# Linear attention and a gated FFN on one core: one written list for the order of all queues, one ring of PSUM banks, loads reordered, zero matmuls at the start

## The chip, the cores and the metric

The kernel runs on one core of a Trainium2 chip. The metric is device time in microseconds of one execution; lower is better. The median of three runs of the kernel before is 246.35 us (245.84 to 247.32). A core has TensorE (PE, matmuls), VectorE (DVE), ScalarE (ACT), GpSimd (POOL) and SyncE (SP). Each runs its own queue of instructions in order; they meet through semaphores. Here POOL issues the loads that have to be cast to fp16 on their way (and some others), SP the remaining loads, the DMA transposes and the stores.

## What is computed

```python
# q, k, v: (8, 8, 576, 64) float32
q_s = softmax(q, axis=-1)            # over the 64 features
k_s = softmax(k, axis=2)             # over the 576 positions
kv  = einsum('bhsd,bhse->bhde', k_s, v)
att = einsum('bhsd,bhde->bhse', q_s, kv)
x   = att.transpose(0, 2, 1, 3).reshape(4608, 512)
h   = (x @ w1) * (x @ w2)            # w1, w2: (512, 1024)
out = (h @ w3) @ w_out               # w3: (1024, 1024), w_out: (1024, 512)
```

## The kernel before, in words

**Fold.** w3 @ w_out is computed once (W3O, 1024 x 512), so that the second half of the FFN is one product. For each of eight row blocks `ft`: `w3t.ft` transposes eight 128x128 blocks of w3 on TensorE (L441), `w3T.ft` copies them from PSUM to SBUF, `pf.ft.0` and `pf.ft.1` are two times four matmuls with w_out (L451), and `W3O.ft` evicts the sum.

**Attention, for each batch b.** Steps are named by their kind, the batch and a part:
- `kmx`, `cb`: maximum of k over the positions, on VectorE (L479, or a tree at L488 to L491 in batches 0 and 1; `cb` is L495 to L506). `ksub` (L537) subtracts it, `kexp` is the exponential on ScalarE. There are two halves, `.0` and `.1`.
- `vc` casts v to fp16 (batches 2 to 7). In batches 0 and 1 the load casts.
- `kv` is the product of k's exponentials and v on TensorE (L562, L571), `kv2` its normalisation (L580 to L583).
- `qmx` (L590), `qsub` (L595), `qexp` (L603), `qsm` (L608), `qeps`, `qrc` (L620), `qn` (L627): softmax of q in two parts of 4 and 5 groups of positions (`.0` and `.1`).
- The result is transposed: in batches 0 and 1 on TensorE (`qt`, L642) with an eviction `qT`; from batch 2 on by a DMA transpose that SP issues (`qd`, L650).
- `xm.b.0`, `xm.b.1`, `xt.b`: the attention output on TensorE (L668), on 64x64 tiles; `xs` and `xts` evict it to x. `xt` is the last 64 of the 576 positions. They are gathered over all batches into a ninth chunk.

**FFN, for each chunk c of 512 tokens** (chunks 0 to 7 are the batches, chunk 8 the gathered rest): eight times `up.1.c` (x with w2) and `up.0.c` (x with w1), four 512-column matmuls each (L793); `bs` copies the first from PSUM, `ab` (L808) multiplies it with the second. Then `down.c.0` to `down.c.3`, eight matmuls each with W3O (L815, L830 in chunk 8), evicted by `os` and stored by `st`. Chunk 1 is split in two halves of 256 tokens.

**Order.** No scheduler of the language is used: `Plan` (L18 to L163) holds all steps with an estimated length, what they need, and rings of buffers, places them by list scheduling with the priorities in `LEADS`, picks the engine of the steps that have a choice from `PICKS`, and emits them in the order that comes out. Each engine gets its instructions in that order. PSUM's eight banks are three pools: four `pab` (up, w3t), two `po` (down, pf), two `att` (kv, qt, xm, xt). A step that takes a bank waits until the step that had it last has been evicted.

**Loads.** `LOADS` (L241) is the order of the first loads. `q.0.0` goes on SP, all others on POOL's queue, where the ninth and each later one waits for the eighth before it. From batch 2 on, k, q and v are loaded on SP, in the order k, q, v for each batch, into the two buffers of each tensor. `k.2` waits in addition for `w1.2`, the second-last load of `LOADS`, and since SP's queue runs in order, all behind it do. Sizes as read in fp32: `q.b.0` 0.52 MB, `q.b.1` 0.66, whole `q.b`, `k.b`, `v.b` 1.18, `w3.4`, `w3.5` (two row blocks each), `wo.0`, `wo.1` 1.05, `w3.0` to `w3.3` and each column quarter of w1 and w2 0.52.

Of the kernel before, what the change touches and what calls it, by code (L numbers as in the profile page):

```python
# [17 lines left out]
class Plan:  # L18


    RATE = 409.0e3
    LAND = 1.7
    HOP = 0.15
    NEAR = 0.2
    LINKED = 50.0
    BUS = 2.2
    BEGIN = {"SP": 0.74, "POOL": 1.25, "DVE": 1.0, "ACT": 1.0, "PE": 1.0}

    def __init__(self, rings, leads, picks):
# [6 lines left out]
    def key(name):


        if name[0] == "up":
            return f"up{name[1]}_{min(name[2], 3)}"  # L40
        if len(name) > 2 and name[1] < 2 and name[0] not in ("bs", "ab", "down", "os", "st", "pf"):
            return "_".join(str(x) for x in name)
        return f"{name[0]}_{min(name[1], 3) if len(name) > 1 else 0}"

    @staticmethod
    def group(name):

        return f"{name[0]}_{min(name[1], 3)}_" + "_".join(str(x) for x in name[2:])

    def add(self, name, eng, length, emit, needs=(), lead=0.0, takes=None, gives=(), size=0,  # L50
            slack=0.0, after=(), port=False, slots=1):
        assert name not in self.steps, name
        choices = None
        if isinstance(eng, dict):

            choices = eng
            eng = self.picks.get(self.group(name))
            if eng not in choices:
                eng = next(iter(choices))
            length, port = choices[eng]  # L60
            act = emit
            emit = lambda eng=eng: act(eng)
        self.steps[name] = dict(name=name, eng=eng, length=length, emit=emit, needs=list(needs),
                                lead=lead, takes=takes, gives=list(gives), size=size, slack=slack,
                                after=list(after), port=port, slots=slots, choices=choices)

    def tails(self, users):
        tail = {}
        for first in self.steps:
            stack = [first]  # L70
            while stack:
                n = stack[-1]
                if n in tail:
                    stack.pop()
                    continue
                todo = [u for u, _ in users.get(n, ()) if u not in tail]
                if todo:
                    stack += todo
                    continue
                s = self.steps[n]  # L80
                own = s["length"] + (self.LAND + s["size"] / self.RATE if s["size"] else self.HOP)
                tail[n] = own + max([tail[u] if whole else tail[u] - own
                                     for u, whole in users.get(n, ())], default=0.0)
                stack.pop()
        return tail

    def order(self):
        steps = self.steps
        free = dict(self.BEGIN)
        ends = {}  # L90
        fifo = {tag: [] for tag in self.rings}
        given = {}
        users = {}
        for s in steps.values():
            for taken in s["gives"]:
                given.setdefault(taken, []).append(s["name"])
            s["open"] = len(s["needs"]) + len(s["after"])
            s["at"] = 0.0
            for n in s["needs"]:
                users.setdefault(n, []).append((s["name"], True))  # L100
            for n in s["after"]:
                users.setdefault(n, []).append((s["name"], False))
        tail = self.tails(users)
        for rank, n in enumerate(sorted(steps, key=str)):
            steps[n]["rank"] = -rank
        for s in steps.values():
            s["worth"] = tail[s["name"]] + s["lead"] + self.leads.get(self.key(s["name"]), 0.0)
        ready = [s for s in steps.values() if not s["open"]]
        bus = self.BUS
        port, holder = -9.0, None  # L110
        order = []
        while ready:
            could = {}
            for s in ready:
                at = max(free.get(s["eng"], 0.0), s["at"])
                if s["port"]:
                    at = max(at, port + (self.HOP if holder != s["eng"] else 0.0))
                if s["takes"]:
                    ring = fifo[s["takes"]]
                    last = [n for old in range(len(ring) - self.rings[s["takes"]],  # L120
                                               len(ring) - self.rings[s["takes"]] + s["slots"])
                            if old >= 0 for n in given.get(ring[old], ())]
                    if any(n not in ends for n in last):
                        continue
                    at = max([at] + [ends[n] + self.HOP for n in last])
                could.setdefault(s["eng"], []).append((at, s))
            assert could, "the plan is stuck"
            eng = min(sorted(could), key=lambda e: min(at for at, _ in could[e]))
            soon = min(at for at, _ in could[eng]) + self.NEAR
            at, s = max(((at, s) for at, s in could[eng] if at <= soon),  # L130
                        key=lambda c: (math.floor((c[1]["worth"] - c[0]) * 1e6 + 0.5), c[1]["rank"]))
            ready.remove(s)
            if s["takes"]:
                fifo[s["takes"]] += [s["name"]] * s["slots"]
            free[eng] = at + s["length"]
            if s["port"]:
                port, holder = at + s["length"], s["eng"]
            end = at + s["length"]
            if s["size"]:
                bus = max(bus, at + 0.7) + s["size"] / self.RATE  # L140
                end = bus + self.LAND
            ends[s["name"]] = end
            order.append((at, s))
            for n, whole in users.get(s["name"], ()):
                u = steps[n]
                hop = self.HOP + u["slack"] if u["eng"] != s["eng"] or s["size"] else 0.0
                u["at"] = max(u["at"], end + hop if whole else at)
                u["open"] -= 1
                if not u["open"]:
                    ready.append(u)  # L150
        assert len(order) == len(steps), sorted(set(steps) - set(ends), key=str)[:5]
        return order, ends

    def run(self, link):

        held = None
        for at, s in self.order()[0]:
            got = s["emit"]()
            if s["port"] and at < self.LINKED:
                assert got, s["name"]  # L160
                if held and held[0] != s["eng"]:
                    link(got[0], held[1])
                held = s["eng"], got[-1]  # L163


LEADS = {
# [767 lines left out]
```

## Time and profile before

| | kernel before |
|---|---|
| median of three runs | 246.35 us |
| the profiled execution | 244.56 us |
| its span in the profile | 242.7 us |
| PE busy | 227.2 us, 94% of the span |
| DVE busy | 180.3 us, 74% |
| ACT busy | 120.4 us, 50% |
| POOL busy | 118.2 us, 49% |
| HBM read, written | 38.80 MB, 9.44 MB |

The profile is one execution. In the row of slices each digit is the busy share, in tenths, of one of 40 equal slices of some 6.1 us. The chain that ended last follows back, from the last instruction, what each step waited for. In a timeline the columns are start, length (us), engine, line, operation, output<-inputs, count, and in brackets the idle time of the engine ahead of it and what ended it. The groups of instructions by line give counts and mean lengths, and the rows of DMA issues the median time from issue to landing.

### The profile page before, as it was taken

The page shows a single profiled execution, that of the slowest core. Times are in us where ns is not written, and L with a number is a line of the kernel's source. Part 1 is how long each engine was busy: PE and PEld are TensorE (multiplying, and loading weights), DVE is VectorE, ACT ScalarE, POOL GpSimd, SP SyncE. Part 2 cuts the span into 40 slices and gives each one's busy share as a digit, 9 for nine tenths or more (in the row PEclk, how much of TensorE's full clock was granted, in tenths as well). Part 3 has the DMA queues.
Part 4 walks back from the last instruction along what each step waited for, and adds up shares of the span by engine and source line. Part 5 has one row for each costly group of instructions (what it writes and reads, how often), then busy time and mean ns, then how long its engine had stood idle before and what let it go on. Part 6 is the DMA issues. An engine that isn't in the chain of part 4 may idle for free.

```text
span 242.7 us, 4757 instructions
## 1 busy us (share of the span) xinstructions
PE 227.2 (94%) x1884; PEld 112.1 (46%) x1884; DVE 180.3 (74%) x306; ACT 120.4 (50%) x183; POOL 118.2 (49%) x79
## 2 busy tenths in 40 slices
PE   0398899999999999999999999999999999999994
...
DVE  2889869969998989989998999799876154335320
...
DMA  6999999999998994993999089801940230022153
GB/s 229 234 265 251 260 298 196 248 398 391 354 151 292 388 171 123 399 219 67 324 384 177 0 309 375 173 4 36 131 108 3 58 72 0 3 64 66 43 130 130
DMA packets 37766, 45.65 MB, mean 188 GB/s; under 512 B 15985, under 2 KB 21873, under 8 KB 37745
## 3 DMA queue, kind: packets, MB, share of 16 engines
...
HBM read 38.80 MB, written 9.44 MB: 199 GB/s over the span
## 4 chain that ended last, share of the span: by engine, by line
PE 90%; DMA 6%; POOL 2%; issue 1%; ACT 1%; ACTq 0%; POOLq 0%
PE pab L793 52%; PE po L815 23%; DMA w<-in_moe_w_dram 6%; PE po L451 4%; PE po L830 3%; PE pkv L562 2%; PE xm L668 2%; PE w3t L441 1%; PE xt L668 1%; PE qtp L642 1%; POOL w L403 1%; PE pkv L571 1%; ACT w3T L342 0%; POOL wosb L403 0%; POOL k L403 0%
## 5 line engine op out<-in xcount | busy, mean ns | idle before, releaser
L808 DVE TENSOR_TENSOR ab<-pab,bsb 128x512 f16<-128x512 f32 x72 | 49.0, 687 | 24.8 <-PE pab L793 19.3
L793 PE MATMUL pab<-x,w2sb 128*128 128x512 f16 (+1 forms) x288 | 65.9, 356 | 0.0
L793 PE MATMUL pab<-x,w1sb 128*128 128x512 f16 (+1 forms) x288 | 65.9, 356 | 0.0
L815 PE MATMUL po<-W3O,ab 128*128 128x512 f16 x256 | 59.3, 380 | 0.0
L342 ACT CAST bsb<-pab 128x512 f16<-128x512 f32 x49 | 28.5, 582 | 40.6 <-PE pab L793 40.5
L793 PEld LDWEIGHTS <-w1sb 128*128 128x128 f16 x320 | 30.7, 98 | 30.0
L793 PEld LDWEIGHTS <-w2sb 128*128 128x128 f16 x320 | 30.5, 98 | 29.3 <-issue 0.2
L537 POOL TENSOR_TENSOR k<-k,cb 128x1152 f32<-128x1152 f32 x14 | 36.5, 2623 | 10.5 <-issue 7.9
L627 POOL TENSOR_TENSOR en<-eq,qr 128x1024 f16<-128x1024 f16 (+1 forms) x14 | 29.3, 2096 | 21.9 <-issue 9.1
L815 PEld LDWEIGHTS <-ab 128*128 128x128 f16 x256 | 23.8, 98 | 29.7 <-issue 2.9
L595 POOL TENSOR_TENSOR q<-q,qm 128x1280 f32<-128x1280 f32 (+1 forms) x13 | 27.7, 2145 | 13.7 <-DVE rc L580 11.7
L342 ACT COPY osb<-po 128x512 f32<-128x512 f32 (+1 forms) x28 | 15.9, 569 | 35.8 <-PE po L815 31.0
L479 DVE TENSOR_REDUCE km<-k 128x128 f32<-128x1152 f32 x12 | 25.8, 2149 | 0.0
L590 DVE TENSOR_REDUCE qm<-q 128x16 f32<-128x1024 f32 (+1 forms) x16 | 21.5, 1345 | 5.7 <-DMA q<-in_q_dram 5.7
L603 ACT ACTIVATE eq<-q 128x1024 f16<-128x1024 f32 (+1 forms) x16 | 18.6, 1164 | 13.7 <-POOL q L595 6.9
L545 ACT ACTIVATE ek<-k 128x1152 f16<-128x1152 f32 x16 | 18.6, 1163 | 6.5 <-POOL k L537 5.1
L608 DVE TENSOR_REDUCE qr<-eq 128x16 f32<-128x1024 f16 (+1 forms) x16 | 21.2, 1324 | 0.1
L342 DVE CAST bsb<-pab 128x512 f16<-128x512 f32 x23 | 15.8, 685 | 5.2 <-PE pab L793 4.0
L451 PE MATMUL po<-wosb,w3T 128*128 128x512 f16 x64 | 16.8, 408 | 1.2 <-issue 0.6
L346 ACT ACTIVATE x<-xm 128x512 f16<-128x512 f32 x30 | 16.5, 598 | 1.7 <-PE xm L668 1.7
L441 PE MATMUL w3t<-ident,w 128*128 128x128 f16 x64 | 5.8, 249 | 11.0 <-DMA w<-in_moe_w_dram 11.0
L342 ACT COPY w3T<-w3t 128x1024 f16<-128x1024 f16 x8 | 8.0, 1016 | 6.4 <-PE w3t L441 5.9
...
## 6 DMA issues: line engine op xcount, KB each, us to landing
...
```

The lines of the kernel that those rows point to most:

```text
L342: return [(nc.scalar.copy if eng == "ACT" else engine[eng].tensor_copy)(out=out, in_=in_)]
L451: nc.tensor.matmul(st["pf", ft], lhsT=st["w3T", ft][:, gt, :], rhs=wosb[:, gt, :], start=(gt == 0), stop=(gt == N_FT - 1))
L479: dve.tensor_reduce(out=st["km", b][:, two(hp), :], in_=kb[:, two(hp), :, :].rearrange("p h j d -> p h d j"), axis=AX.X, op=ALU.max)
L537: return [engine[eng].tensor_tensor(out=kb[:, two(hp), :, :], in0=kb[:, two(hp), :, :], in1=st["cb", b][:, two(hp), None, :].broadcast_to( ...
L545: nc.scalar.activation(out=st["ek", b][:, hp, :, :].rearrange("p j (i d) -> p i j d", i=2), in_=kb[:, two(hp), :, :], func=AF.Exp)
L590: dve.tensor_reduce(out=st["qm", b][:, :, j], in_=qb[:, :, j, :], axis=AX.X, op=ALU.max)
L595: return [engine[eng].tensor_tensor(out=qb[:, :, j, :], in0=qb[:, :, j, :], in1=st["qm", b][:, :, j, None].broadcast_to([P, HH, n, D]), op ...
L608: dve.tensor_reduce(out=st["qr", b][:, :, slice(*PARTS[p])], in_=st["eq", b, p], axis=AX.X, op=ALU.add)
L627: return [engine[eng].tensor_tensor(out=st["en", b][:, j, :, :].rearrange("p j h d -> p h j d"), in0=st["eq", b, p], in1=st["qr", b][:, :, ...
L793: nc.tensor.matmul(st["p", one, c, sub, u][:, a * (t1 - t0):(a + 1) * (t1 - t0)], lhsT=w[:, ct, fb * P:(fb + 1) * P], rhs=x()[:, ct, t0:t1 ...
L808: dve.tensor_tensor(out=st["ab", c][:, nf * u:nf * u + nf, t0:t1], in0=cut(st["p", 0, c, sub, u]), in1=cut(st["bsb", c, sub, u]), op=ALU.mult)
L815: nc.tensor.matmul(st["po", c, tb], lhsT=st["ab", c][:, ft, tb * P:(tb + 1) * P], rhs=W3O[:, ft, :], start=(ft == 0), stop=(ft == N_FT - 1))
```

## The change

- `Plan` loses its estimates, its priorities and its list scheduling. `ORDER` is a written list of all steps, with a letter for the engine where there is a choice (A, D, P), and `run` emits the steps in that order. Semaphores between DVE and POOL on the steps marked `port`, before only for steps planned to start within 50 us, are now set up to the last such step on DVE.
- One pool of eight banks, one tag, in place of 4 + 2 + 2.
- Loads: the order is that of `ORDER`. POOL: `w3.4 q.0.1`, the identity matrix, `k.0 wo.0 wo.1 w3.0 w3.2 w3.3 q.1.0 v.0 w3.5 q.1.1 w2.0 w3.1 w1.0 k.1 w2.1 w1.1 w2.2 w1.2 w2.3 w1.3 v.1`; `GATE` is still `w1.2`, on `k.2`. SP: `q.0.0 q.2 k.2 v.2 v.3`, the stores of `os.0.0`, `k.3 q.3 q.4 v.4 k.4`, and so on.
- 13 matmuls on a zeroed tile (`zero.0`) are the first on TensorE. VectorE clears the tile.
- The second identity matrix (fp32) and the unused code for a maximum on TensorE are gone. `qn.0.0`, `qsub.1.1` and `qn.1.0` move from POOL to VectorE, among other moves between engines.

```diff
-    pab_pool = ctx.enter_context(tc.tile_pool(name="pab", bufs=4, space=bass.MemoryType.PSUM))
-    po_pool = ctx.enter_context(tc.tile_pool(name="po", bufs=2, space=bass.MemoryType.PSUM))
-    att_pool = ctx.enter_context(tc.tile_pool(name="att", bufs=2, space=bass.MemoryType.PSUM))
-    plan = Plan({"pab": 4, "po": 2, "att": 2, "osb": 4, "eq": 4, "bsb": 4, "w3T": 2}, LEADS, PICKS)
+    banks = ctx.enter_context(tc.tile_pool(name="banks", bufs=8, space=bass.MemoryType.PSUM))
+    plan = Plan({"ps": 8, "osb": 4, "eq": 4, "bsb": 4, "w3T": 2})
...
+    ZEROS = [13]
...
+    zero = konst.tile([P, 512], F16)
+    dve.memset(zero, 0.0)
+
+    def zeros(i, n):
+        def go():
+            st["zero", i] = bank([P, 512], F32, "zero")
+            for _ in range(n):
+                nc.tensor.matmul(st["zero", i], lhsT=zero[:, 0:P], rhs=zero, start=True, stop=True)
...
+    for name in LOADS:
+        load(name, "SP" if name in EARLY else "POOL")
+    for b in range(2, B):
+        for n in "kqv":
+            load((n, b), "SP", GATE if (n, b) == ("k", 2) else None)
...
-    plan.run(link)
+    plan.run(ORDER, link)
```

The new class's `run`, and the list up to batch 2 (the list goes on in the same form to the last store):

```python
    def run(self, order, link):
        byname = {self.text(n): s for n, s in self.steps.items()}
        listed = [t.partition("/")[::2] for t in order.split()]
...
        held = None
        for i, (t, code) in enumerate(listed):
            s = byname[t]
            eng = s["eng"]
            if isinstance(eng, tuple):
                eng = self.CODES[code]
                assert eng in s["eng"], t
                got = s["emit"](eng)
            else:
                got = s["emit"]()
            if s["port"] and eng != "ACT" and held and i <= twos[-1] and held[0] != eng:
                link(got[0], held[1])
            if s["port"] and eng != "ACT":
                held = eng, got[-1]

EARLY = [("q", 0, 0)]
GATE = ("w1", 2)

ORDER = """
zero.0 q.0.0 qmx.0.0 qsub.0.0/D w3.4 q.0.1 ident w3t.5 w3t.4 k.0 qexp.0.0 qsm.0.0 qeps.0.0/D qmx.0.1 w3T.5/A
w3T.4/A qrc.0.0 qsub.0.1/D qn.0.0/D qt.0.0 wo.0 pf.4.0 qexp.0.1 wo.1 pf.5.0 pf.5.1 w3.0 w3t.0 w3T.0/A pf.4.1
kmx.0.0 cb.0 qsm.0.1 ksub.0.0/D qeps.0.1/D ksub.0.1/D W3O.5/A W3O.4/A w3.2 w3t.2 w3T.2/A pf.0.0 w3.3 w3t.3
pf.0.1 qT.0.0/A pf.2.0 pf.2.1 w3T.3/A pf.3.0 pf.3.1 q.1.0 kexp.0.1 v.0 kexp.0.0 kv.0 W3O.0/A W3O.2/A w3.5
w3t.6 qmx.1.0 qrc.0.1 w3t.7 qn.0.1/D qt.0.16 qt.0.8 w3T.7/A qsub.1.0/D qexp.1.0 W3O.3/D w3T.6/D pf.6.0 pf.6.1
W3O.6/A kv2.0 qT.0.8/D qT.0.16/D xm.0.0 xs.0.0.0/A xs.0.0.1/A xm.0.1 xs.0.1.0/A xt.0 xs.0.1.1/A q.1.1 qmx.1.1
qsub.1.1/D qsm.1.0 qeps.1.0/D qrc.1.0 pf.7.0 pf.7.1 w2.0 up.1.0.0.0 w3.1 w3t.1 w1.0 up.0.0.0.0 up.1.0.0.1
w3T.1/A xts.0.1/A xts.0.0/A pf.1.0 pf.1.1 k.1 bs.0.0.0/D qn.1.0/D ab.0.0.0 kmx.1.0 w2.1 W3O.7/A up.0.0.0.1
up.1.0.0.2 qexp.1.1 bs.0.0.1/A ab.0.0.1 cb.1 w1.1 up.0.0.0.2 up.1.0.0.3 up.0.0.0.3 bs.0.0.3/A W3O.1/A
bs.0.0.2/A ab.0.0.2 qsm.1.1 qeps.1.1/A qrc.1.1 ab.0.0.3 w2.2 up.1.0.0.4 bs.0.0.4/A w1.2 up.0.0.0.4 ab.0.0.4
up.1.0.0.5 up.0.0.0.5 bs.0.0.5/A w2.3 up.1.0.0.6 bs.0.0.6/A w1.3 up.0.0.0.6 up.1.0.0.7 up.0.0.0.7 qt.1.0
ab.0.0.5 ab.0.0.6 v.1 ksub.1.0/P kexp.1.0 ksub.1.1/P kexp.1.1 kv.1 qn.1.1/P qt.1.8 qt.1.16 qT.1.0/A qT.1.8/A
bs.0.0.7/D ab.0.0.7 down.0.0 q.2 qmx.2.0 kv2.1 qT.1.16/D qmx.2.1 qsub.2.1/P qsub.2.0/P xm.1.0 xs.1.0.0/A
xm.1.1 xt.1 down.0.1 xs.1.0.1/A os.0.0/A up.1.1.0.0 xs.1.1.1/A qexp.2.1 xs.1.1.0/A xts.1.1/A bs.1.0.0/A
os.0.1/A xts.1.0/A k.2 kmx.2.1 kmx.2.0 qsm.2.1 cb.2 v.2 v.3 st.0.0 k.3 q.3 up.0.1.0.0 up.1.1.0.1 up.0.1.0.1
up.1.1.0.2 bs.1.0.2/A up.0.1.0.2 up.1.1.0.3 up.0.1.0.3 qeps.2.1/D ab.1.0.0 bs.1.0.1/A ab.1.0.2 ab.1.0.1
vc.3.0/P bs.1.0.3/A ab.1.0.3 qexp.2.0 qsm.2.0 qeps.2.0/A up.1.1.1.0 down.1.0 up.0.1.1.0 up.1.1.1.1 down.0.2
down.0.3 q.4 vc.2.0/A vc.2.1/P v.4 bs.1.1.0/D qrc.2.0 kmx.3.0 qmx.3.0 qrc.2.1 ab.1.1.0 kmx.3.1 ksub.2.1/P
kexp.2.1 ksub.2.0/P kexp.2.0 kv.2 k.4 st.0.1 os.1.0/A os.0.2/A up.0.1.1.1 up.1.1.1.2 up.0.1.1.2 kv2.2
bs.1.1.1/D cb.3 ab.1.1.1 os.0.3/A bs.1.1.2/A up.1.1.1.3 up.0.1.1.3 bs.1.1.3/A down.1.1 qmx.3.1 ab.1.1.2
qn.2.0/P qn.2.1/P qd.2.1 st.0.2 qd.2.0 xm.2.0
"""
```

More of the change, by code (lines that the diff above doesn't have):

```diff
@@ L18, with __init__ @@
 class Plan:
[L21 to L29, printed above, removed]
+    CODES = {"A": "ACT", "D": "DVE", "P": "POOL"}
+    def __init__(self, rings):
         self.rings = rings
-        self.leads = leads
-        self.picks = picks
         self.steps = {}
-    @staticmethod
[L36 to L152, printed above, removed]
@@ L154, in run, with add @@
-    def run(self, link):
-        held = None
[L157 to L166, printed above, removed]
[36 rows of a table removed]
-}
-PICKS = {
[31 rows of a table removed]
-}
+    def add(self, name, eng, emit, needs=(), takes=None, gives=(), size=0, kind="", late=(),
+            port=False, slots=1):
+        assert name not in self.steps, name
+        self.steps[name] = dict(name=name, eng=eng, emit=emit, needs=list(needs), takes=takes,
+                                gives=list(gives), size=size, kind=kind, late=list(late), port=port,
+                                slots=slots)
@@ new lines @@
+qn.2.0/P qn.2.1/P qd.2.1 st.0.2 qd.2.0 xm.2.0 st.1.0 xs.2.0.0/A xs.2.0.1/A os.1.1/A xm.2.1 ab.1.1.3 down.1.2
+kmx.4.1 xs.2.1.1/A xs.2.1.0/D down.1.3 up.1.2.0.0 up.0.2.0.0 up.1.2.0.1 vc.3.1/P qsub.3.0/P qexp.3.0 qsm.3.0
+qeps.3.0/D ksub.3.1/P qsub.3.1/P qexp.3.1 q.5 qrc.3.0 qsm.3.1 qmx.4.1 kmx.4.0 bs.2.0.1/A bs.2.0.0/A ab.2.0.0
+os.1.3/A os.1.2/A up.0.2.0.1 ab.2.0.1 up.1.2.0.2 up.0.2.0.2 up.1.2.0.3 up.0.2.0.3 up.1.2.0.4 bs.2.0.2/A
+ksub.3.0/P qn.3.0/P qd.3.0 qsub.4.1/P kexp.3.1 kexp.3.0 bs.2.0.3/A ab.2.0.2 qeps.3.1/A qrc.3.1 qn.3.1/P qd.3.1
@@ new lines @@
+bs.3.0.1/A qeps.4.0/A qeps.5.0/A os.2.0/A qsub.5.1/P qexp.5.1 down.2.2 os.2.2/D ab.3.0.1 up.0.3.0.2 up.1.3.0.3
+up.0.3.0.3 up.1.3.0.4 ab.3.0.2 st.1.2 st.2.1 q.6 v.6 bs.3.0.3/A bs.3.0.4/A up.0.3.0.4 up.1.3.0.5 bs.3.0.5/A
+up.0.3.0.5 up.1.3.0.6 up.0.3.0.6 up.1.3.0.7 kmx.5.0 qrc.5.0 qeps.4.1/A ksub.4.1/P kexp.4.1 ksub.4.0/P kexp.4.0
+k.6 ab.3.0.3 qsm.5.1 qeps.5.1/D ab.3.0.5 qrc.4.1 qn.4.1/P vc.5.1/P qrc.4.0 qn.4.0/P ab.3.0.4 kmx.5.1 xt.2
+xts.2.0/D kv.4 bs.3.0.6/A up.0.3.0.7 qd.4.1 st.2.0 qd.4.0 q.7 down.2.3 os.2.3/A ab.3.0.6 xts.2.1/D bs.3.0.7/D
@@ new lines @@
+ab.3.0.7 down.3.0 os.3.0/A st.3.0 down.3.1 qn.5.0/P os.3.1/A st.3.1 st.2.2 kv2.4 xm.4.1 qrc.5.1 cb.5
+xs.4.1.0/A xm.4.0 xs.4.1.1/A qmx.6.1 xs.4.0.0/D xs.4.0.1/A down.3.2 os.3.2/A st.3.2 up.1.4.0.0 bs.4.0.0/A
+up.0.4.0.0 up.1.4.0.1 up.0.4.0.1 up.1.4.0.2 up.0.4.0.2 qsub.6.1/P qexp.6.1 kmx.6.1 bs.4.0.2/D bs.4.0.1/A
+ab.4.0.0 qmx.7.0 ab.4.0.1 ab.4.0.2 up.1.4.0.3 up.0.4.0.3 bs.4.0.3/D ab.4.0.3 up.1.4.0.4 qn.5.1/P ksub.5.1/P
+vc.6.1/A ksub.5.0/P st.2.3 qd.5.0 qd.5.1 qsub.7.0/P v.7 bs.4.0.4/A kexp.5.0 up.0.4.0.4 up.1.4.0.5 down.3.3
@@ new lines @@
+up.0.4.0.5 bs.4.0.5/A qmx.6.0 qsub.6.0/P qmx.7.1 ab.4.0.4 up.1.4.0.6 up.0.4.0.6 ab.4.0.5 qsm.6.1 up.1.4.0.7
+bs.4.0.7/D up.0.4.0.7 kexp.5.1 os.3.3/A qexp.6.0 bs.4.0.6/A ab.4.0.6 st.3.3 k.7 xt.4 xts.4.0/A xts.4.1/D
+qeps.6.1/D ab.4.0.7 kv.5 kv2.5 down.4.0 os.4.0/A st.4.0 down.4.1 os.4.1/A kmx.6.0 xm.5.0 xs.5.0.1/A xm.5.1
+xt.5 down.4.2 down.4.3 qexp.7.0 xs.5.1.1/A os.4.2/A cb.6 qrc.6.1 xs.5.1.0/D xs.5.0.0/D xts.5.1/D qsm.7.0
+qeps.7.0/A kmx.7.1 up.1.5.0.0 up.0.5.0.0 ksub.6.1/D bs.5.0.0/D ab.5.0.0 os.4.3/D st.4.3 st.4.2 xts.5.0/A
@@ new lines @@
+up.1.5.0.1 bs.5.0.1/A up.0.5.0.1 up.1.5.0.2 up.0.5.0.2 up.1.5.0.3 up.0.5.0.3 bs.5.0.2/D ab.5.0.2 qsub.7.1/P
+qexp.7.1 qsm.6.0 bs.5.0.3/A qeps.6.0/A qn.6.1/P ksub.6.0/P vc.6.0/P st.4.1 qd.6.1 ab.5.0.1 up.1.5.0.4
+up.0.5.0.4 up.1.5.0.5 ab.5.0.3 qsm.7.1 up.0.5.0.5 up.1.5.0.6 up.0.5.0.6 kexp.6.1 bs.5.0.4/A ab.5.0.4
+bs.5.0.6/D qrc.6.0 ab.5.0.6 bs.5.0.5/D ab.5.0.5 kexp.6.0 up.1.5.0.7 up.0.5.0.7 bs.5.0.7/A ab.5.0.7 qn.6.0/P
+qd.6.0 kv.6 kmx.7.0 kv2.6 down.5.0 down.5.1 xm.6.0 xs.6.0.1/A xs.6.0.0/A xm.6.1 xs.6.1.1/D xs.6.1.0/A os.5.0/A
@@ L248 @@
+down.8.3.0 os.8.3.0/D st.8.3.0 down.8.3 os.8.3/A st.8.3
+"""
 @with_exitstack
@@ L688, in attention @@
-        if PEMAX[b]:
-            A(("kmt", b), "PE", 0.25, kmt, kms + [("ident32",)], takes="att", slack=SLACK)
-            A(("mx", b), "DVE", 0.9, mx, [("kmt", b)], gives=[("kmt", b)])
-            A(("kmb", b), "PE", 0.25, kmb, [("mx", b)], takes="att", slack=SLACK)
-            A(("cb", b), {"ACT": (0.38, False), "DVE": (0.4, False)}, 0, cbp, [("kmb", b)],
-              gives=[("kmb", b)])
-        else:
-            A(("cb", b), "DVE", 2.25, cb, kms)
+                A(("kmx", b, hp), "DVE", lambda hp=hp: kmx_one(hp), [("k", b)])
```

265 lines of the change are left out of this document (119 added, 146 removed), and 67 rows, old and new, of tables (LEADS, PICKS).

## The prediction

> **What bounds the kernel now.** I read the page first: the span in slices and the chain that ended last.
>
> ```profile
> PE   0398899999999999999999999999999999999994
> DVE  2889869969998989989998999799876154335320
> DMA  6999999999998994993999089801940230022153
> PE 90%; DMA 6%; POOL 2%; issue 1%; ACT 1%; ACTq 0%; POOLq 0%
> ```
>
> TensorE is full from the sixth slice to the last; what is not TensorE in the chain is one DMA wait at the start. VectorE is nearly full too up to about 180 us, so it has little room for a worse order. Next, the timeline up to 32 us.
>
> ```profile
> 9.92 1.93 PE L441 MATMUL w3t<-ident,w 128*128 128x128 f16 x16 [9.92 <-DMA w<-in_moe_w_dram]
> 12.39 1.87 PE L451 MATMUL po<-wosb,w3T 128*128 128x512 f16 x4 [0.55 <-DMA wosb<-in_moe_w_out_dram]
> ...
> 13.62 2.13 PE L451 MATMUL po<-wosb,w3T 128*128 128x512 f16 x5
> ...
> 19.02 0.72 PE L441 MATMUL w3t<-ident,w 128*128 128x128 f16 x8 [1.04 <-DMA w<-in_moe_w_dram]
> ...
> 30.05 1.67 PE L451 MATMUL po<-wosb,w3T 128*128 128x512 f16 x7 [0.57 <-issue]
> ```
>
> TensorE idles until 9.92, runs at about 0.43 us per 512-column matmul until some 15.7 (2.13/5), at 0.216 later (8 in 1.73), waits for weights until 19.02, and from 30.05 to the end of its last matmul at 239.36 has no gap. So 209.3 us of gapless work follow 30.05, and **only two things can move the end: how much TensorE work is done by some early time, and gaps or fewer transitions later.** Third, what sets the loads, from the timelines of each engine and SP's waits.
>
> ```profile
> 7.59 1.23 DVE L488 TENSOR_TENSOR kmx<-k 128x1024 f32<-128x1024 f32 x1 [0.52 <-DMA k<-in_k_dram]
> ...
> 17.92 1.49 DVE L590 TENSOR_REDUCE qm<-q 128x20 f32<-128x1280 f32 x1 [0.77 <-DMA q<-in_q_dram]
> ```
>
> ```profile
> 44.59 0.39 SPq L403 DMA_DIRECT2D k<-in_k_dram  x1
> ```
>
> Each of these starts when a load lands. In order of issue, with bytes read in fp32 (q.0.0 0.52 MB, k.0 1.18, w3.4 1.05, ...), k.0 lands at 7.59 with 1.70 MB read, w3.4 at 9.92 with 2.75, q.0.1 at 17.92 with 6.03, w1.2 (SP's gate) at 44.59 with 16.4. That is a straight line, 0.39 MB/us: the loads are one stream at full rate, and I take each landing of the new order from its cumulated bytes.
>
> **The change, part by part.**
>
> *Load order.* New cumulated bytes give: w3.4 7.2 us, q.0.1 8.9, k.0 11.8, wo.0 14.1, wo.1 16.7, w3.0 17.9, w3.2 19.0, w3.3 20.5, q.1.0 21.5, v.0 24.5, w3.5 27.1, q.1.1 29.9, w2.0 31.2, w3.1 32.3, w1.0 33.5, k.1 36.4, w2.1 37.7, w1.1 39.0, w2.2 40.3, w1.2 41.6, w2.3 43, w1.3 44.3, v.1 47.2.
>
> *q.2 leaves its gate.* In the old order SP has q.0.0, then k.2, which waits for w1.2 (43.3 us of waiting on SP), and q.2 behind it. In the new order q.2 comes ahead of k.2, and the gate is still on k.2 alone. q.2 then waits only for its buffer, that is for qexp.0.1. On VectorE: q.0.0 lands 4.6; qmx.0.0 and qsub.0.0 (1.22 each) to 7.1, qsm.0.0 behind qexp.0.0 to 9.4, qeps, qmx.0.1, qrc to 11.3, qsub.0.1 to 12.7; qexp.0.1 (1.27 on ScalarE) ends at 14.0. So 1.18 MB start to flow at about 16, in the middle of the weights: 1.18/0.39 = 3.0 us. Bounds: 0 (it uses only gaps) and 3.0 for every load behind it; I take 3.0, because the stream has no gaps from 7.6 to 44.6.
>
> *Fold on TensorE.* The new order has qt.0.0 behind the first 16 transposes. It waits for qn.0.0, now on VectorE (1.2 for POOL's 1.91), done at 13.9. Until then TensorE has done 0.9 us of its work; the old order had done four and a half matmuls of pf more. From there: qt.0.0 and pf.4.0, 5.0, 5.1 at the slow rate to 19.9; w3t.0, pf.4.1 to 21.2; w3.2 and w3.3, late by 2.5 to 3.0, hold w3t.2 to 21.6 and w3t.3 to 23.4; pf.0.1, 2, 3 to 28.2; kv.0 (1.44) to 29.8; w3.5 at 30.1 to 30.4; w3t.6, 7, three qt, pf.6 to 33.7 (VectorE: W3O.3, w3T.6, kv2.0, two qT end at 33.4); xm.0, xt.0, pf.7 to 36.4; xs on ScalarE to 36.4; up.1.0.0.0, w3t.1, up.0.0.0.0, up.1.0.0.1, pf.1 (1.7), up.0.0.0.1, up.1.0.0.2 (0.87 each) to 43.0, where w1.1 (42) is there. Without q.2's 3.0 us the same walk gives 41.2.
>
> By 43.0 the new order has done 8 w3t (3.6), 16 half pf (13.8), qt.0 (1.0), kv.0 (1.4), xm.0 and xt.0 (0.9) and five up (4.3): 25.1 us. The old one had done 14.5 at 30.05 (7 w3t, 41 matmuls of pf, qt.0, kv.0) and 12.5 more by 43.0: 27.0. **New order behind by 1.95 us.**
>
> *Matmuls on zeros.* 13 at 0.43 is 5.6 us, from VectorE's memset at about 1.5 to 7.1, all under the wait for w3.4: nothing on the path. What they buy: bounds 0 and 2.85 us (half of the 5.7 us slow time). TensorE is idle from 8.1 to 13.9, and no row of before shows a fast stretch that survives such a gap, so I take 0. Under q.2's delay even full speed gains nothing, since w3.3 and w3.5 set the times. The Trainium skill ("TensorE: Matmul & The Clock Gate", section "What's actually happening") says that the clock falls to half after about 3.4 us of idling; by that rule these zeros are lost again, which speaks against this part. Nothing above needs the rule.
>
> *One ring of eight banks.* No TensorE wait for a bank stands in the waits of before, so no stall goes. But with two att banks xm.b.0 and xm.b.1 had to stand apart, and each step on 64-row tiles costs a transition:
>
> ```profile
> 98.87 0.34 PE xm L668 x4
> 99.21 1.83 PE po L815 x8
> ...
> 120.22 3.56 PE po L815 x16
> ```
>
> Eight matmuls beside an xm take 1.83; of sixteen, the second eight take 3.56 - 1.83 = 1.73. A transition is 0.10. In the new order xm.b.0 and xm.b.1 are adjacent in batches 1 to 7 (7 fewer), xt joins xm in 1, 3, 5, 7 (4) and kv in 2, 4, 6 (3): 14 x 0.10 = **1.4 us gained.**
>
> *v.1.* The gate w1.2 now stands ahead of w2.3, w1.3 and v.1. At 44.6 k.2 and v.2 (2.4 MB) start and flow from 46.6; v.1, else at 50.2, shares the stream and lands near 54.3. TensorE is at kv.1 at 43.0 + 10.0 = 53.0. **Gap 1.3 us** (bounds 0 and 3).
>
> *Batch 2.* From kv.1 at 54.3 VectorE runs kv2.1, qT.1.16, qmx.2.1, two kmx.2 (2.15), qsm, cb.2 to 66.2, then qeps, four ab, qsm.2.0, bs, qrc.2.0, kmx.3.0, qmx.3.0, qrc.2.1 to 74.1; POOL's qn.2.1 (2.34) to 76.5; two DMA transposes on SP with a store between them, 4.3 to landing, to 83.2. TensorE is at xm.2.0 at 82.6. **Gap 0.6 us** (bounds 0 and 3). In before qn.2 ended at 69 and xm.2 came at 77.9: 9 us of cover, now none. Later batches gain cover: POOL ends qn.3.1 at 94.4, and xm.3 is due at 102.
>
> *Rest.* ident32 gone (0.5 us of POOL), more osb and x evictions on VectorE (0.69 for 0.58 on ScalarE): hidden by VectorE's idle time after 180. The tail's last eviction stays a 256-column one on ScalarE (0.37) and its store.
>
> **Sum:** 1.95 - 1.4 + 1.3 + 0.6 = +2.45. The profiled execution took 244.56 us (span 242.7), 1.8 under the median of 246.35; the difference is added to either: 247.0 for a run like that one, 248.8 for the median.
>
> **Rivals.**
> 1. *q.2 costs no load time* (it fills gaps, or the weights keep precedence). For: no row shows an SP load beside eight of POOL's at that place. Against: no gap in the stream. The place is 16 to 24 us; decisive is whether w3t.3 can start before 21.5. Then 43.0 becomes 41.2, 1.95 becomes 0.15, the sum -1.25 with no gap at kv.1 and -0.65 or less with that of batch 2: 245.1 to 245.7, not slower.
> 2. *VectorE's order bites harder.* kmx.3.0 and qmx.3.0 stand ahead of qrc.2.1 and wait for k.3 and q.3, which SP issues only behind v.3 (after kv.1) and a store, near 61.5. With the 5.8 and 9.3 us to landing of the profile's DMA rows they come at 67 and 71, needed at 70.8 and 72.9. If q.3 is 4 us later than that, qrc.2.1 and xm.2 move by 2.5 us: 251.3.
> 3. *The clock stays up from the zeros on, and q.2 is free.* Then pf.5.1 ends at 17.8 instead of 19.9, w3.5 (27.1) sets the pace and 0.9 more is gained: 244.2.
>
> **How the numbers follow.** The forecast has 0.45 (slower 0.40, within 0.05), rival 1 0.30 (faster 0.13, within 0.17), rival 2 0.13 (slower), rival 3 0.07 (faster), gaps elsewhere in a list with little cover 0.05 (slower 0.04, within 0.01). A measurement of this kernel tells about 0.5%, 1.2 us. Range: 244.8, most of rival 1 with it, to 251.3, rival 2.
>
> **What would show it.** q.2's issue on SP at 14 to 15 us, and w3t.3 starting after 23; the five pf halves before 20 us at 0.43 per matmul; up.0.0.0.2 at 43; a TensorE wait ahead of kv.1 near 53 and ahead of xm.2 near 82; TensorE gapless after 85 to about 241.8. Wrong if q.2 is issued behind w1.2, if TensorE at 43 us is beyond up.0.0.0.2, or if gaps stand after 85 us.

## The result, and the profile after

The changed kernel takes 255.62 us (median of four runs, 254.06 to 256.16) against 246.09 us for the kernel before on the same chip: a ratio of 1.037, 95% interval 1.031 to 1.044, so slower. The forecast was 248.8 us, its range ended at 251.3. The profiled execution took 254.06 us, its span is 252.3 us. The rows of the page that answer to those of before:

```profile
PE   7288699999999399989997999999999999999994
...
DVE  3896699899999476898998499999865572536452
...
PEclk9979999999999779999999999999999999999999
DMA  7999999987999834598979798108214443005313
...
PE 54%; DMA 16%; DVE 16%; issue 5%; POOL 4%; SPq 2%; ACT 1%; DVEq 0%; POOLq 0%; ACTq 0%
```

The 3 in TensorE's row at the 14th slice (82 to 88 us) is new, and the granted clock falls in that slice and the next (7 and 7; the 7 in the third slice stands behind the wait of `qt.0.0`). VectorE (4) is half idle in that slice too; the DMA engines are still at 8 in it and fall to 3 and 4 behind it. TensorE's share of the chain is 54% where it was 90%. TensorE's own waits name the place (engine, step, what it waited for: total, times, longest):

```profile
PE xm L507 <- DMA qT<-en: 5.8, 2, 5.0
...
PE xm L507 <- DVE qm L429: 1.6, 1, 1.6
```

and the timeline of TensorE there (start, length, ..., idle time ahead of it):

```profile
79.48 1.89 PE L639 MATMUL po<-W3O,ab 128*128 128x512 f16 x8
86.33 1.07 PE L507 MATMUL xm<-qT,kv 64*64 64x512 f16 x8 [4.96 <-DMA qT<-en]
87.33 5.64 PE L639 MATMUL po<-W3O,ab 128*128 128x512 f16 x16
92.81 1.03 PE L617 MATMUL pab<-x,w2sb 128*128 128x512 f16 x4
```

The other long wait, 5.2 us at `qt.0.0`, was in the forecast. The wait of 4.96 us ahead of `xm.2.0` was forecast with 0.6. Behind it, the eight matmuls of `xm.2` take 1.07 us where later `xm` take 0.63, and the 16 of `down.1.2` and `down.1.3` take 5.64 us where later runs of 16 take 3.63 (109.08, for instance). What `xm.2` waits for stands on SP's queue:

```profile
70.25 0.37 SPq L287 DMA_DIRECT2D v<-in_v_dram  x1
72.33 0.37 SPq L287 DMA_DIRECT2D k<-in_k_dram  x1
...
75.37 3.25 SPq L489 DMA_TRANSPOSE qT<-en  x1
78.72 1.17 SPq L665 DMA_DIRECT2D out_dram<-osb  x2
79.95 2.42 SPq L489 DMA_TRANSPOSE qT<-en  x1
```

`v.4` and `k.4`, 2.4 MB together, are issued ahead of the two transposes. `qd.2.1` takes 3.25 us to issue and lands 9.4 us after its start; `qd.2.0` starts at 79.95, takes 2.42, and lands at 86.25.

**Where the time went.** TensorE's last matmul ends at 249.0 (239.36 before), 9.6 us later:

| term | forecast | measured |
|---|---|---|
| TensorE behind at the front | +1.95 | +2.3: `up.0.0.0.3` starts at 45.02; before 43.18, with 0.45 of `qt.1.0` done in addition |
| transitions | -1.4 | -3.1 (14 at 0.22, from the eleventh experiment) |
| gap at `kv.1` | +1.3 | 0 |
| gap at `xm.2` | +0.6 | +5.0 |
| slow clock behind it | 0 | +2.5 (from `xm.2` to `up.1.2.0.0` 6.48; 4.02 in experiments 3 and 5) |
| gaps at `xm.3`, `xm.4`, `xm.6` | 0 | +2.6 (0.83, 1.61, 0.19) |
| sum | +2.45 | +9.3 |

The remaining 0.3 us isn't assigned. The trace is that of the fastest of the four runs: its mean granted clock is 0.979, that of the others 0.964 to 0.973, so they ran longer at the slow clock than the table has it; where, is not on record.

### The profile page after: what moved, and what is told of

Same layout as the page of the kernel before. It is cut to its first block, busy times and chain, and to the rows that moved or that the text cites. A ratio compares the mean times of both kernels' runs of the same rounds, so it can differ in the third digit from the quotient of the medians.

```text
span 252.3 us, 4752 instructions
## 1 busy us (share of the span) xinstructions
PE 231.0 (92%) x1897; PEld 115.3 (46%) x1897; DVE 190.4 (75%) x325; ACT 107.3 (43%) x167; POOL 113.1 (45%) x75
## 4 chain that ended last, share of the span: by engine, by line
PE 54%; DMA 16%; DVE 16%; issue 5%; POOL 4%; SPq 2%; ACT 1%; DVEq 0%; POOLq 0%; ACTq 0%
PE pab L617 33%; PE po L639 13%; DMA w<-in_moe_w_dram 7%; DVE ab L632 4%; DVE km L345 3%; DMA k<-in_k_dram 3%; DMA out_dram<-osb 3%; DVE qr L447 3%; PE po L654 3%; DMA qT<-en 2%; PE pf L317 2%; PE xm L507 2%; POOL q L434 2%; DVE qm L429 1%; DVE bsb L218 1%
## 5 line engine op out<-in xcount | busy, mean ns | idle before, releaser
L632 DVE TENSOR_TENSOR ab<-pab,bsb 128x512 f16<-128x512 f32 x72 | 47.4, 679 | 12.2 <-PE pab L617 11.1
L218 ACT CAST bsb<-pab 128x512 f16<-128x512 f32 x47 | 27.1, 589 | 53.9 <-PE pab L617 53.6
L376 POOL TENSOR_TENSOR k<-k,cb 128x1152 f32<-128x1152 f32 x13 | 34.0, 2626 | 18.5 <-DVE cb L372 8.8
L466 POOL TENSOR_TENSOR en<-eq,qr 128x1280 f16<-128x1280 f16 (+1 forms) x13 | 27.8, 2141 | 27.8 <-DVE qr L459 20.1
L434 POOL TENSOR_TENSOR q<-q,qm 128x1280 f32<-128x1280 f32 (+1 forms) x12 | 25.4, 2125 | 8.3 <-DVE qm L429 7.5
L218 ACT COPY osb<-po 128x512 f32<-128x512 f32 (+1 forms) x22 | 12.5, 580 | 30.5 <-PE po L639 16.5
L222 ACT ACTIVATE x<-xm 128x512 f16<-128x512 f32 x24 | 13.3, 603 | 20.4 <-PE xm L507 20.4
L218 DVE COPY osb<-po 128x512 f32<-128x512 f32 (+1 forms) x15 | 10.1, 670 | 10.4 <-PE po L639 6.8
L317 PE MATMUL pf<-wosb,w3T 128*128 128x512 f16 x64 | 15.9, 397 | 0.0
L218 POOL CAST v<-v 128x1152 f16<-128x1152 f32 x8 | 10.2, 1286 | 6.5 <-DMA v<-in_v_dram 6.5
```

What stands on the lines that cost most here:

```text
L218: return [(nc.scalar.copy if eng == "ACT" else engine[eng].tensor_copy)(out=out, in_=in_)]
L317: nc.tensor.matmul(st["pf", ft], lhsT=st["w3T", ft][:, gt, :], rhs=wosb[:, gt, :], start=(gt == 0), stop=(gt == N_FT - 1))
L376: return [engine[eng].tensor_tensor(out=kb[:, two(hp), :, :], in0=kb[:, two(hp), :, :], in1=st["cb", b][:, two(hp), None, :].broadcast_to( ...
L434: return [engine[eng].tensor_tensor(out=qb[:, :, j, :], in0=qb[:, :, j, :], in1=st["qm", b][:, :, j, None].broadcast_to([P, HH, n, D]), op ...
L466: return [engine[eng].tensor_tensor(out=st["en", b][:, j, :, :].rearrange("p j h d -> p h j d"), in0=st["eq", b, p], in1=st["qr", b][:, :, ...
L632: dve.tensor_tensor(out=st["ab", c][:, nf * u:nf * u + nf, t0:t1], in0=cut(st["p", 0, c, sub, u]), in1=cut(st["bsb", c, sub, u]), op=ALU.mult)
```

## The experiments

Each kernel is the changed kernel with steps moved in `ORDER`, unless said otherwise; lines keep their numbers. "After" is the changed kernel, "before" the kernel before. Beside the runs before had medians of 246.28 (1 to 4), 246.43 (5 to 8), 246.12 (9 to 11) and 245.24 us (12).

**1. The loads of batch 4 behind the transposes of batch 2.**

```diff
-vc.2.1/P v.4 bs.1.1.0/D
+vc.2.1/P bs.1.1.0/D
...
-kv.2 k.4 st.0.1
+kv.2 st.0.1
...
-qd.2.1 st.0.2 qd.2.0 xm.2.0
+qd.2.1 st.0.2 qd.2.0 v.4 k.4 xm.2.0
```

> v.4 and k.4 are moved in the list to behind qd.2.0, nothing else changes. Theory A (the two loads, 2.4 MB or about 6 us of the load stream, stand on SP ahead of batch 2's DMA transposes and hold them, and the gap they make on TensorE also lets the clock fall): qd.2.0 lands within 4.5 us of its issue, the gap ahead of xm.2 shrinks from 4.96 us to under 1, the 16 matmuls behind it take 3.6 us and not 5.6, and the span falls by 6 to 8 us to about 245. Rival B (the transposes are late because qn.2 is late on POOL and because they are slow by themselves): qd.2.1's issue still takes over 3 us, the gap stays over 4 us and the time within 1 us of the changed kernel's.

Measured: 256.87 us, ratio 1.044 (1.039 to 1.048). The first lines are TensorE's, the last two VectorE's:

```profile
81.97 0.63 PE L507 MATMUL xm<-qT,kv 64*64 64x512 f16 x8 [0.71 <-DMA qT<-en]
82.53 3.63 PE L639 MATMUL po<-W3O,ab 128*128 128x512 f16 x16
...
92.53 1.01 PE L617 MATMUL pab<-x,w2sb 128*128 128x512 f16 x2 [5.93 <-DVE x L224]
```

```profile
89.76 2.12 DVE L345 TENSOR_REDUCE km<-k 128x128 f32<-128x1152 f32 x1 [7.46 <-DMA k<-in_k_dram]
91.79 0.68 DVE L224 TENSOR_SCALAR x<-xm 128x512 f16<-128x512 f32 x1
```

The place of the loads does make the gap at `xm.2` (4.96 becomes 0.71), and without the gap the 16 matmuls take 3.63 us. But the time did not fall, where theory A had 6 to 8 us less: `kmx.4.1` stands in VectorE's order ahead of the eviction `xs.2.1.0`, and with `k.4` later VectorE stands still for 7.46 us, and TensorE for 5.93. The list holds `k.4` from two sides.

**2. In addition q.2 behind the gate** (`k.2` ahead of `q.2`).

> As e1, and k.2 put ahead of q.2 in the list, so that SP's gate on w1.2 holds q.2 as in the kernel before. Theory A (q.2's 1.18 MB take 3.0 us from the weights): w3t.3 starts near 21 and not 22.5, the first up.0 of the third pair (43.29 in the changed kernel) starts near 41.3, and the end comes up to 1.9 us earlier than in e1. Rival B (the time by which TensorE is ahead at 43 us is lost again at batch 2, whose chain starts with k.1, k.2 and q.2): the front moves by 1.9 us, but the gap ahead of xm.2 grows by as much, and the time is within 0.6 us of e1's. Rival C: q.2 costs nothing, w3t.3 does not move.

Measured: 256.25 us, ratio 1.042 (1.037 to 1.046). `up.0.0.0.2` starts at 41.10 (experiment 1: 43.19; after: 43.29), so `q.2` did cost the front 2.1 us. But `w3t.3`, expected near 21, starts at 22.43 (after: 22.54), and without a wait: the 12 matmuls of `pf` ahead of it stayed at the slow rate and took 5.33 us (after: 3.69). The gain comes behind it, where after's waits for `v.0` and `w3.5` (1.00 and 0.93) are gone. Of the 2.1 us 0.6 reach the median: gaps of 0.37 at `xm.1`, 0.43 at `down.0.2` and 1.81 at `xm.2` take their place, and that of 5.56 behind them stays.

**3. Matmuls on zeros in the gap** (L503: 22 of them into `xm.2.0`'s bank ahead of it; everything else as after).

> The changed kernel with 22 matmuls on zeros (4.75 us at full speed) put on TensorE ahead of xm.2's first real one, into the bank that xm.2 overwrites: the gap of 4.96 us is filled without being shortened. Theory A (the gap drops the clock to half for 5 us, which costs 2.1 us by itself): the 16 matmuls of down.1.2 and down.1.3 take 3.6 us, the granted clock has no 0.5 stretch after 80 us, and the time falls by about 2 us. Rival B (the matmuls behind the gap are slow because their weights or operands come late): they still take over 5 us and the time is within 0.6 us of the changed kernel's or above.

Measured: 254.86 us, ratio 1.035 (1.025 to 1.045).

```profile
81.17 4.91 PE L503 MATMUL xm<-zero 128*128 128x512 f16 x22
...
86.58 3.63 PE L639 MATMUL po<-W3O,ab 128*128 128x512 f16 x16
```

The transposes land no earlier, `xm.2` still starts at 86.02, but the 16 matmuls take 3.63 and `up.1.2.0.0` starts at 90.04 instead of 92.81. So the idle time alone, and nothing about the data, lowers the clock. Most of these 2.8 us is lost again: `xm.4` waits 2.49 instead of 1.61, and this time the clock falls behind it, for 3.4 us at half speed. The four runs spread from 252.99 to 257.14, so the median, 0.8 lower, shows nothing; the trace does.

**4. No zeros at the start** (`ZEROS = []`).

> The changed kernel without the 13 matmuls on zeros. Theory A (they warm the clock for the first 16 transposes only, which wait for nothing behind them, and TensorE's 5.2 us of idling lose it again): the 16 transposes take 1.9 us for 1.2, qt.0.0 still starts at 13.6, and the time is within 0.6 us of the changed kernel's. Rival B (the zeros save part of the slow time after 13.6): the pf steps behind 13.6 run at the slow rate 2 us longer or more and the time rises by 1 to 2 us.

Measured: 254.44 us, ratio 1.033 (1.027 to 1.039).

```profile
7.02 1.93 PE L307 MATMUL w3t<-ident,w 128*128 128x128 f16 x16 [7.02 <-DMA w<-in_moe_w_dram]
```

The first 16 transposes take 1.93 us (after: 1.21), but `qt.0.0` starts at 13.71 (13.62), and the 12 matmuls of `pf` behind take 3.96 (3.69). The zeros buy nothing, as forecast: they lie ahead of a wait that does not move.

**5. As 1, and kmx.4.1 directly ahead of kmx.4.0.**

```diff
-kmx.4.1 xs.2.1.1/A xs.2.1.0/D
+xs.2.1.1/A xs.2.1.0/D
...
-qmx.4.1 kmx.4.0
+qmx.4.1 kmx.4.1 kmx.4.0
```

> The first experiment (v.4 and k.4 behind qd.2.0 on SP) with the maximum kmx.4.1 moved in the list to directly ahead of kmx.4.0, so that VectorE does not stand still at k.4 with the eviction xs.2.1.0 behind it. Theory A (the changed kernel's loss is the 5.0 us gap ahead of xm.2 and the 2.1 us of slow clock behind it, both made by the place of v.4 and k.4 in the list): the gap ahead of xm.2 stays at some 0.7 us, that of 5.9 us ahead of up.1.2.0.0 is gone, the 16 matmuls of down.1.2 and down.1.3 take 3.6 us, and the median is 255.6 - 4.3 - 2.1 = 249.2 us (248.0 to 250.5). Theory B (the list has no slack around batches 2 to 4, and a step moved in it only moves the stop): another gap of over 2 us opens behind xm.2, and the median stays above 252 us.

Measured: 249.26 us (248.07 to 251.48), ratio 1.014 (1.007 to 1.020).

```profile
81.82 0.63 PE L507 MATMUL xm<-qT,kv 64*64 64x512 f16 x8 [0.58 <-DVE ab L632]
82.38 3.63 PE L639 MATMUL po<-W3O,ab 128*128 128x512 f16 x16
...
102.52 0.63 PE L507 MATMUL xm<-qT,kv 64*64 64x512 f16 x8 [1.86 <-DMA qT<-en]
```

Theory A: 249.2 was expected. Three moved steps give back 6.4 of the 9.5 us. That the number was met so closely is partly luck: the gap gave 4.4 and the clock 2.5, and 1.1 went to longer waits at `xm.3` (1.86 for 0.83) and `xm.6` (0.30 for 0.19). On SP `qd.2.1` now takes 1.43 us, and its data land in 3.7 (experiment 1: 1.43 and 5.2).

**6. As 5, with q.2 behind the gate.**

> The kernel before this one (v.4 and k.4 behind qd.2.0, kmx.4.1 later) with k.2 ahead of q.2 on SP, so that q.2 waits for w1.2 and takes nothing from the first loads. Theory A (the 1.9 us by which the front was late count in full once the gaps are gone): up.0.0.0.2 starts at 41.1 to 41.5 in place of 43.3, and the median is 1.5 to 2 us under that of the kernel before this one, some 247.3 us. Theory B (the attention steps of batches 2 to 4 are not earlier, so TensorE only waits longer for them): front as in A, but the gaps ahead of xm.1 to xm.4 grow by as much, and the median is within 0.7 us of the kernel before this one.

Measured: 248.31 us, ratio 1.009 (1.006 to 1.012). `up.0.0.0.2` starts at 41.02, 2.15 us earlier than in 5. The median is 0.95 lower, between the two theories; the traces speak for B: TensorE's gaps behind 43 us sum to 6.5 us where 5 had 4.4.

**7. v.4 and k.4 on POOL's queue** (`load((n, b), "POOL" if (n, b) in (("v", 4), ("k", 4)) else "SP", ...)`, `k.4` moved behind `qn.2.0`).

> The changed kernel with v.4 and k.4 issued on POOL's queue in place of SP's, v.4 at its place in the list and k.4 directly behind qn.2.0, so at the same times as in the changed kernel (70.3 and 72.4 us, give or take 1 us). Theory A (the transposes qd.2.1 and qd.2.0 are late because they stand behind 2.4 MB of loads in the same queue): their issue takes 1.2 to 1.8 us instead of 3.25 and 2.42, the gap ahead of xm.2 is 0.5 to 1.5 us, the clock stays up, and the median is 249 to 251 us. Theory B (they are late because the DMA engines are busy with those bytes, whatever queue they come from): issue and landing as in the changed kernel, a gap of 3.5 to 6 us, and the median within 1.2 us of 255.6.

Measured: 256.04 us, ratio 1.044 (1.037 to 1.052). This run doesn't answer the question: POOL stood 6.87 us at `v.4`, which waits for the cast `vc.2.0` on ScalarE, and held `kv.2` by 3.58. Only the loads' issue on SP was to change, and with it POOL's work was changed.

**8. Before, with one ring of eight banks** (the three pools become one, tag `ps`; order and engines of before).

> The kernel before with one part of the change alone: one pool of eight PSUM banks with one tag in place of 4 + 2 + 2, every step in the order and on the engine it has in the kernel before. Theory A (no wait for a bank stood on TensorE's path, and a ring by itself changes nothing; what was gained came from putting xm and xt together): the median is within 0.5 us of the kernel before, 246.1. Theory B (banks given in turn make TensorE wait for slow evictions of kv, qt or xm that stand between those of up): TensorE's idle time behind 31 us grows from about nothing to over 1 us, and the median is 247.3 us or more.

Measured: 246.29 us against 246.43, ratio 1.000 (0.997 to 1.004). Theory A: the ring by itself is worth nothing.

**9. As 7, v.4 behind ksub.2.0.**

> The run with v.4 and k.4 on POOL again, without its flaw: there POOL stood 6.9 us at v.4, which waits for a cast on ScalarE, and held kv.2 and the rest. Now v.4 stands behind ksub.2.0 on POOL and k.4 behind qn.2.0 as before, so the 2.4 MB start at some 70.6 and 73 us, as they do in the changed kernel, and qn.2.1 ends about 1 us later than there, near 76.4. Theory A (the transposes stand behind 2.4 MB in their own queue): the issue of qd.2.1 takes 1.3 to 1.8 us instead of 3.25, its landing 3.5 to 5.5 us instead of 9.4, the gap ahead of xm.2 is 1.5 to 3 us, and the median 250 to 252.5 us. Theory B (the DMA engines are busy with those bytes, whatever the queue): issue over 2.5 us and landing over 7.5 us as in the changed kernel, a gap of 4.5 us or more, and the median within 1.2 us of 255.6 or above.

Measured: 251.65 us, ratio 1.022 (1.020 to 1.024). SP's queue and TensorE:

```profile
76.50 1.94 SPq L489 DMA_TRANSPOSE qT<-en  x1
...
80.39 1.33 SPq L489 DMA_TRANSPOSE qT<-en  x1
```

```profile
84.01 0.63 PE L507 MATMUL xm<-qT,kv 64*64 64x512 f16 x8 [2.75 <-DMA qT<-en]
84.57 5.31 PE L639 MATMUL po<-W3O,ab 128*128 128x512 f16 x16
```

Theory A, with issue and landing a little over its bounds. The loads start 0.4 and 1.0 us later than in after and `qd.2.1` 1.1 us later, and yet it takes 1.94 instead of 3.25 and lands in 5.8 instead of 9.4; `qd.2.0` lands in 3.5 instead of 6.3. So most of the delay comes from standing behind those bytes in the same queue. What is left over 1.43 and 3.7 (experiment 5) or 5.2 (experiment 1) may be the shared DMA engines; that wasn't taken apart further. The clock falls here too.

**10. Four gaps closed** (as 6, and):

```diff
-qmx.2.0 kv2.1 qT.1.16/D
+kv2.1 qT.1.16/D qmx.2.0
...
-qn.2.0/P qn.2.1/P qd.2.1 st.0.2 qd.2.0
+qn.2.0/P qd.2.0 qn.2.1/P qd.2.1 st.0.2
...
-qsm.3.1
+qsm.3.1 qeps.3.1/D qrc.3.1
...
-qsm.4.1
+qsm.4.1 qeps.4.1/D qrc.4.1
...
-qrc.5.0
+qrc.4.0 qrc.5.0
...
-qd.4.1 st.2.0 qd.4.0
+qd.4.1 qd.4.0 st.2.0
```

> The kernel with v.4 and k.4 behind the transposes, kmx.4.1 later and q.2 behind the gate (248.3 us), and the steps moved that its trace shows ahead of its other gaps: kv2.1 and qT.1.16 ahead of qmx.2.0; qd.2.0 directly behind qn.2.0; qeps.3.1 and qeps.4.1 on VectorE instead of ScalarE, each with its qrc directly behind qsm; qrc.4.0 ahead of qrc.5.0; qd.4.0 ahead of st.2.0. Theory A (each of the four gaps, 0.85 us at xm.1, 1.45 at xm.2, 1.68 at xm.3 and 1.92 at xm.4, hangs on the one late step that its own row shows): all four are under 0.3 us and the median is 248.3 - 5.9 = 242.4 us (241.5 to 244), under that of the kernel before, 246.4. Theory B (VectorE, POOL and SP are full in 50 to 130 us, and what is late moves to another step): over 2 us of gaps are left or new, and the median is above 245 us.

Measured: 247.22 us, ratio 1.005 (1.002 to 1.008). Three of the four gaps are gone, that at `xm.4` is 0.38; but 1.46 us are new at 94 us (`up` waits for a bank behind two `kmx` of 4.26 us on VectorE), and small ones bring the listed gaps to 3.6 us. Theory B: of the 5.9 us 1.1 were won in the median, 0.8 when each is taken against its own runs of before (248.31 - 246.43 and 247.22 - 246.12).

**11. As 10, six transitions back** (batches 5 to 7: a `down` step between `xm.b.0`, `xm.b.1` and `xt`).

> The kernel of this call with its gaps closed, but in batches 5 to 7 the attention steps stand apart again on TensorE, with a down step between: xm.5.0, xm.5.1 and xt.5; xm.6.0 and xm.6.1; xt.6 behind down.6.0 and not behind kv.7; xm.7.1, xm.7.0 and xt.7. Six more changes from 64x64 tiles to whole 128x128 tiles and back. Read from the trace, from the first matmul of down.4.0 to the last of TensorE. Theory A (the price of the prediction, 0.10 us each): 0.6 us longer. Theory B (0.16 each, which is what 2.3 us for 14 of them would be): 0.9 to 1.0 us longer. The median is up by as much, if no new wait comes with the moved steps.

Measured: 251.67 us, ratio 1.024 (1.019 to 1.030); two waits came with the moved steps (1.67 at `xm.6.0`, 0.89 at `up.1.7.0.0`), so the price is read from the trace. First 10, then 11, around batch 7:

```profile
198.04 0.63 PE L507 MATMUL xm<-qT,kv 64*64 64x512 f16 x8
```

```profile
198.16 0.41 PE L507 MATMUL xm<-qT,kv 64*64 64x512 f16 x4
198.50 1.90 PE L639 MATMUL po<-W3O,ab 128*128 128x512 f16 x8
200.33 0.41 PE L507 MATMUL xm<-qT,kv 64*64 64x512 f16 x4
```

From the first matmul of `down.4.0`, at 147.24 in both, to the end 10 takes 94.78 us with 0.61 of waits, 11 takes 98.04 with 2.56: 1.31 us for six, **0.22 each**. That is more than either theory had. The 0.10 of the prediction is one part: eight matmuls beside an `xm` take 1.83 for 1.73. The other part stands in the `xm` itself: four matmuls alone take 0.34 from start to start (198.16 to 198.50), so 0.68 in two pieces, where eight in one piece take 0.45 (198.04 to 198.49, where `xt` begins). A divided `xm` so costs 0.33, and an `xt` set apart little more than the 0.10.

**12. Two more gaps** (as 10; `kmx.4.1` behind `ab.2.0.1`, `kmx.4.0` behind `ab.2.0.3`, `bs.2.0.7` on ScalarE).

> The kernel with its four gaps closed (247.2 us, ratio 1.005 to the kernel before), with the two steps moved that its trace shows ahead of what was left at batch 2 and 3: kmx.4.1 behind ab.2.0.1 and kmx.4.0 behind ab.2.0.3 on VectorE, where both stood in one piece of 4.26 us ahead of four ab steps (gap of 1.46 us at 94.3), and the copy bs.2.0.7 on ScalarE instead of VectorE (0.19 and 0.35 us, and 0.57 us by which the row of xm.3 is longer than the others). Theory A (those are the late steps): the gap at 94 us and those at 101 us are under 0.2 us, TensorE ends 2 to 2.5 us earlier, and the median is 244.7 to 245.4 us, a ratio of 0.995 to 0.998, the first of this list under the kernel before. Theory B (VectorE is full there and the stop moves to a later step): gaps of over 1 us stay between 90 and 135 us, and the ratio is 1.003 or more.

Measured: 247.05 us, ratio 1.005 (1.002 to 1.009).

```profile
99.95 1.20 PE L507 MATMUL xm<-qT,kv 64*64 64x512 f16 x8 [1.52 <-DVE kv L422]
...
101.34 5.30 PE L639 MATMUL po<-W3O,ab 128*128 128x512 f16 x16
```

Theory B: the wait at 94 us is gone, but VectorE comes to `kv2.3` at 99 us as it did in 10, so now `xm.3` waits there, and this time the clock fell (5.30 us for 16 matmuls). None of these kernels is faster than before.

## Why the prediction was wrong

The sign was right, the size was not: +9.5 us for +2.45. One row of SP's queue in before belongs to the first point (start, length):

```profile
81.89 3.17 SPq L650 DMA_TRANSPOSE qT<-en  x1
```

- **The failed step is "Batch 2", gap 0.6 us.** It walked VectorE and POOL to 76.5 (measured: `qn.2.1` ends at 75.34, a microsecond early) and TensorE to 82.6 (81.4). Then it took "two DMA transposes on SP with a store between them, 4.3 to landing, to 83.2", 6.7 us after `qn.2.1`. It took 10.9: from the start of the first transpose to that of the second 4.6 us, where the forecast leaves 2.4, and 6.3 to landing for 4.3. The 4.3 is the median of before's transposes, and `v.4` and `k.4`, which the list puts ahead of them on SP (5.1 and 3.0 us in the trace), were not walked past. Experiments 1, 5 and 9 show it. The bounds "0 and 3" came without a row for a transpose behind loads, but before has one, the row above: it lands in 6.3 us, and of the `k`, `q` and `v` issued ahead of it on SP from 72.80 to 73.78, `q` and `v` (9.7 and 12.0 us to landing) are still on their way. The median hid it.
- **What hangs on that gap was left out:** 2.5 us of slow clock (experiment 3). The prediction speaks of a clock that falls after idling, but only for the zeros, where nothing depends on it; the gap of 5.0 us cost 7.4.
- **"Later batches gain cover" is wrong.** The prediction saw `qn.3.1` end by 94.4 and `xm.3` due at 102. `qn.3.1` ran from 101.32 to 103.66, held by `qrc.3.1` behind `qeps.3.1` on ScalarE, and `xm.3`, `xm.4` and `xm.6` wait 2.6 us together. Experiments 6, 10 and 12 show that the list has no slack from 50 to 135 us: each gap closed opens part of another.
- **q.2:** right. SP passes it at 14.1, `w3t.3` starts at 22.54 (forecast 23.4), `up.0.0.0.2` at 43.29 (43.0); experiments 2 and 6 give 2.1 us for putting it back (forecast 1.8). Rival 1 is refuted. One of the signs failed without harm: the first 12 matmuls of `pf` took 0.31 each and not 0.43, and TensorE waited for the loads instead.
- **kv.1:** wrong, 0 for 1.3. `kv.1` follows `qt.1.0` at 53.33 with no wait, so `v.1`, forecast for 54.3, had landed.
- **Transitions:** right in kind and count, wrong in price: 0.22 each for 0.10, so 3.1 us for 1.4. The prediction took the price from the `down` step beside an `xm` and not from the divided `xm`.
- **Zeros and ring at nothing:** right (experiments 4 and 8). Rival 3 is refuted: the granted clock is 0.50 from 13.5 to 14.5 us.
- **Rival 2** names the right wait with the wrong cause: `qrc.2.1` was not late (72.9 for 74.1), the transposes behind it were.

Two things stay open: how the delay of the transposes divides between the queue and the shared DMA engines, and why in 10 TensorE ends 2.5 us later than the terms of the table give for it (239.4 - 0.4 at the front - 3.1 + 3.6 = 239.5; measured 242.0). Of that, 1.6 stands inside rows that are longer than others of their kind (`xm.3` 1.20 for 0.63, `xm.6` 0.82 for 0.63, `xt.2` with `kv.4` 1.11 for 0.81, three `down` 5.58 for 5.35, one `up` 1.31 for 1.03).
